# Local attention and a feed-forward layer on one core: scores in four quarters, first loads from two queues, and an ordering list with other numbers

## Chip, core and metric

One core of a Trainium2 chip. The metric is device microseconds of one launch, median of three runs. The engines named here: PE (TensorE; PEld is its weight load), DVE (VectorE), ACT (ScalarE), POOL (GpSimd), SP (SyncE, which begins the DMAs). PSUM has eight banks of 128 x 512 fp32 here.

## What is computed

For 8 batches of 8 heads, 576 tokens and 64 features: attention over q, k, v averaged by four, repeated back to full length, plus attention within three tokens to either side; the sum goes through a layer norm and a two-layer ReLU network and is added to its input.

```python
q_d = q.reshape(B, H, Sd, factor, D).mean(axis=3)        # the same for k and v, factor 4
out_up = np.repeat(sm_attn(q_d, k_d, v_d), factor, axis=2)
mask = np.abs(pos[:, None] - pos[None, :]) < factor
scores = np.where(mask, scale * np.matmul(q, k.transpose(0, 1, 3, 2)), -1000000000.0)
out_local = np.matmul(softmax(scores), v)
x = (out_up + out_local)                                 # to (8, 576, 512)
xn = (x - mu) / np.sqrt(var + 1e-06) * g_ln
out = x + np.maximum(xn @ w_ch1, 0.0) @ w_ch2            # 512 -> 2048 -> 512
```

The network's weights come as float64, 16.8 MB, and its products are made in three passes (hi and lo parts of weights and activations).

## The kernel before

**Windows.** The tokens of a batch are cut into five windows of 2 x 58 queries, 40 windows in all, numbered i. A window's two halves (`par` 0 and 1) lie on partitions 0 to 63 and 64 to 127, and each has 64 keys. `local(i)` adds a window's steps: loads of q and k (names qn, kn for windows 0 to 6, which PE transposes; qr, kr for the others, which DVE transposes in 32 x 32 blocks), the load of v into one of two tiles vwin, scores into PSUM (tile ls), mask, maximum (lmx), subtraction, exp (la), a PE transpose (lt, copied out as at), the product with v (lv), the division (xl), and DMAs that move the rows of xl into the token tiles x of 128 rows.

**Scores.** Windows 0 to 6 use `scores_by_pair`, which writes two banks. The others use `scores` (L473): for each of 8 heads and each half, a product of 64 x 64 by 64 whose inputs and outputs both lie on the half's partitions, into one bank.

**Pooled attention.** `pooled(b)` loads q, k, v (raw), adds fours on POOL, and makes scores gs, transposes gq and gt, and the product gv. Batch 0 takes its sums of q and k from the windows' transposes instead.

**Norm and network.** `norm(n)` adds the pooled part to tile x, normalises it and transposes it on PE (px); ACT writes the hi part (xh, L879), DVE the lo part (xlo). `ffn(c, p)` works on 18 chunks of 256 tokens and 8 pairs of weight blocks: 24 products into h, ReLU on ACT (hh) and the rest on DVE (hl), 12 products into acc. Chunks 0 and 1 run side by side while the weights come in. `weights(which, f)` loads a block of w1 or w2 as two tiles s, and turns it into hi and lo with ACT (cva L328, hi L347), DVE (cva L336 and L339) and DVE or POOL (lo L352).

**Order.** Nothing is ordered by hand. Each step is added to a `Plan` with an engine, a duration in us, a due time, the buffers it takes and gives back (`u`: 87 SBUF units, `a`: the 8 PSUM banks), and a `lag` after which its result counts as there (2.9 us for a load). `Plan.order` (L49) places the steps one after another by these numbers, and every engine runs its instructions in that order. An instruction that waits holds up all that stands behind it on its engine. All DMAs are begun by SP.

```python
t = add("PE", 1.28, scores, turned, due - 6.0, take=A, give=(("u", 2),))
last_local.v[i % 2] = tv = add("PE", 1.3, times_v, (at, vt), due - 1.0, take=(("a", 2),), give=U)
vt = add("SP", 4 * DMA, load_v, (last_local.v[i % 2],), due - 8.0, lag=LAT, ahead=AHEAD)
```

Of the kernel before, what the change touches and what calls it, by code (L numbers as in the profile page):

```python
# [22 lines left out]
class Plan:  # L23
# [25 lines left out]
    def order(self):  # L49
# [40 lines left out]
        while left:  # L90
# [45 lines left out]
def attention_then_ffn(  # L136
# [32 lines left out]
    NPE, NPB = 7, 1  # L169
    SEP = {}  # L170
# [135 lines left out]
    def weights(which, f):  # L306
# [49 lines left out]
        t = add("SP", 2 * DMA, load, (), due, take=(("u", 3),), lag=LAT + 1.0, ahead=W_AHEAD)  # L356
# [16 lines left out]
    def local(i):  # L373
# [18 lines left out]
        def load_rows(src, nm):  # L392
            x.raw[nm] = unit([P, H, D], f"{nm}n{i}")
            for par in range(2):
                t0 = window_start(w, par)
                nc.sync.dma_start(  # L396
# [3 lines left out]
        def load_v():  # L400
            for par in range(2):
                t0 = window_start(w, par)
                for h2 in range(2):
                    nc.sync.dma_start(  # L404
# [7 lines left out]
        for src, nm in ((q, "q"), (k, "k")):  # L412
            if by_pe:
# [35 lines left out]
                t = add("SP", 1.46, lambda src=src, nm=nm: load_rows(src, nm), (), due - 12.0, take=U,  # L449
                        lag=LAT, ahead=AHEAD)  # L450
# [6 lines left out]
            else:  # L457
# [9 lines left out]
                for jb in range(2):  # L467
                    ts.append(add("SP", 4 * DMA, lambda src=src, nm=nm, jb=jb: load_blocks(src, nm, jb), ts,
                                  due - 14.0, take=() if jb else U, lag=LAT, ahead=AHEAD))
                turned.append(add("DVE", dve(512), turn, ts, due - 8.0, take=U, give=U))  # L470
        vt = add("SP", 4 * DMA, load_v, (last_local.v[i % 2],), due - 8.0, lag=LAT, ahead=AHEAD)

        def scores():  # L473
            x.ps = psa(f"ls{i}").rearrange("p (h j) -> p h j", h=H)
            for h in range(H):
                for par in range(2):
                    hs = slice(64 * par, 64 * par + 64)
                    nc.tensor.matmul(x.ps[hs, h], lhsT=x.qt[hs, h], rhs=x.kt[hs, h], start=True, stop=True)  # L478
# [21 lines left out]
        def masked():  # L500
            nc.vector.tensor_add(x.ps, x.ps, mask.unsqueeze(1).broadcast_to([P, H, 64]))

        def largest():
            x.mx = work.tile([P, H], F32, tag="lmx", bufs=6, name=f"lmx{i}")
            nc.vector.reduce_max(x.mx, x.ps, axis=AX.X)
            if not by_dve:
                nc.vector.tensor_single_scalar(out=x.mx, in_=x.mx, scalar=-SCALE, op=ALU.mult)
# [13 lines left out]

        def shifted():
            nc.vector.tensor_sub(x.ps, x.ps, x.mx.unsqueeze(2).broadcast_to([P, H, 64]))

        def exps():
            x.a = unit([P, H, 64], f"la{i}")
            if by_dve:
                nc.scalar.activation(x.a, x.ps, AF.Exp, scale=SCALE)
                return
            for h in range(H):  # L530
                nc.scalar.activation(x.a[:, h], x.ps[:, h], AF.Exp, scale=SCALE, bias=x.mx[:, h : h + 1])
# [24 lines left out]
        def times_v():  # L556

            x.pv = [
                psa(f"lv{i}_{h2}")[:, : NPAIR * (D + 1)].rearrange("p (h e) -> p h e", h=NPAIR)
                for h2 in range(2)  # L560
            ]
            for pr in range(NPAIR):
                for h2 in range(2):
                    js = slice(64 * h2, 64 * h2 + 64)
                    for par in range(2):
                        hs = slice(64 * par, 64 * par + 64)
                        nc.tensor.matmul(  # L567
                            x.pv[h2][hs, pr], lhsT=x.at[js, pr, hs], rhs=vwin[js, par, pr], start=True, stop=True
# [20 lines left out]
        if by_pe:  # L589
            t = add("PE", 1.6, scores_by_pair, turned, due - 6.0, take=(("a", 2),), give=(("u", 2),))  # L590
            t = add("DVE", 2 * dve(256) + (2 * dve(256) if by_dve else 0.15), largest_by_pair, (t,), due - 5.0)
            t = add("ACT", 2 * act(256) if by_dve else 1.6, exps_by_pair, (t,), due - 5.0, take=U, give=(("a", 2),))
        else:
            t = add("PE", 1.28, scores, turned, due - 6.0, take=A, give=(("u", 2),))
            t = add("DVE", dve(512), masked, (t,), due - 5.0)
            t = add("DVE", dve(512) + (0 if by_dve else 0.15), largest, (t,), due - 5.0)
            if by_dve:
                t = add("DVE", dve(512), shifted, (t,), due - 5.0)
            t = add("ACT", act(512) if by_dve else 1.28, exps, (t,), due - 5.0, take=U, give=A)
# [446 lines left out]
```

## Time and profile before

| | |
|---|---|
| median of 3 runs | 1099.75 us (1098.24 to 1103.15) |
| profiled execution | 1100.44 us, span of its instructions 1098.7 us |
| mean granted clock of TensorE | 0.977 |
| instructions | 23266 |
| DMA | 105.35 MB in 262572 packets, 206912 of them under 512 B |

An engine's share of busy time is a mean over stages. The profile is read by stage: the first 64 us, in which batch 0 goes through attention; 64 to about 160 us, in which the weights come in and chunks 0 and 1 run; and the rest, in which chunks 2 to 17 run with the attention of later batches between them. In rows of waits the columns are the engine and line that waited, for whom, us in total, times, and the longest.

### The profile page before, as it was taken

How to read it: one execution, taken by the hardware profiler on the slowest of the kernel's cores; microseconds unless marked ns; L12 is line 12 of the kernel's file. 1: busy time of each engine (PE TensorE's matmuls, PEld its weight loads, DVE VectorE, ACT ScalarE, POOL GpSimd, SP SyncE). 2: the span in 40 equal slices, each digit the busy share in tenths (PEclk: the TensorE clock that was granted, in tenths of full speed). 3: DMA queues.
4: the chain of work that ended last, by engine and by line, in shares of the span. 5: the costliest groups of instructions: out<-in, count | busy, mean ns of one | idle time of the engine just before them, and what ended most of it. 6: DMA issues, size and time to landing. Idle time of an engine off the chain costs nothing.

```text
span 1098.7 us, 23266 instructions
## 1 busy us (share of the span) xinstructions
PE 1053.8 (96%) x9182; PEld 943.5 (86%) x9182; DVE 513.2 (47%) x1212; ACT 313.5 (29%) x828; POOL 265.3 (24%) x275
## 2 busy tenths in 40 slices
PE   8887689999999999999999999999999999999998
PEld 6776579989889898999898999898988989898997
DVE  7679774634343453453435443544424453534211
ACT  5466443322322222232212131322212232212100
POOL 2313565142214140041132322131400500100000
PEclk9689789999999999999999999999999999999999
DMA  7599754364424344234252525333532333311000
GB/s 161 119 246 258 182 135 116 74 148 95 78 71 113 73 109 88 72 81 118 57 128 57 132 54 104 75 109 74 128 80 68 83 83 60 81 26 48 9 20 20
DMA packets 262572, 105.35 MB, mean 96 GB/s; under 512 B 206912, under 2 KB 245056, under 8 KB 262464
## 3 DMA queue, kind: packets, MB, share of 16 engines
q1 hardware_dynamic: 262464, 103.87, 40.1%
q8 instruction: 72, 1.18, 0.5%
q14 instruction: 36, 0.29, 0.1%
HBM read 82.58 MB, written 11.80 MB: 86 GB/s over the span
## 4 chain that ended last, share of the span: by engine, by line
PE 82%; DMA 10%; SPq 3%; DVE 3%; issue 1%; ACT 1%; POOL 0%; DVEq 0%; ACTq 0%
PE h L933 34%; PE acc L956 33%; DMA s<-in_moe_w_ch_dram 5%; PE ls L478 3%; DMA x<-xl 3%; PE gv L761 3%; PE lv L567 2%; PE gs L725 2%; SPq L396 1%; PE lt L547 1%; PE gt L744 1%; PE px L872 1%; SPq L404 1%; DMA raw2k<-in_k_dram 1%; PE gq L698 1%
## 5 line engine op out<-in xcount | busy, mean ns | idle before, releaser
L956 PE MATMUL acc<-hi,hl 128*128 128x512 f32 x576 | 238.6, 414 | 5.1 <-DVE hl L944 5.1
L956 PE MATMUL acc<-lo,hh 128*128 128x512 f32 x576 | 229.1, 398 | 0.3 <-DVE lo L352 0.3
L956 PE MATMUL acc<-hi,hh 128*128 128x512 f32 x576 | 227.2, 394 | 0.0
L944 DVE SCALAR_TENSOR_TENSOR hl<-h,hh 128x512 fp32r<-128x512 f32 x144 | 98.9, 687 | 265.4 <-ACT hh L940 235.4
L940 ACT ACTIVATE hh<-h 128x512 fp32r<-128x512 f32 x144 | 86.1, 598 | 428.7 <-PE h L933 376.7
L933 PE MATMUL h<-xh,lo 128*128 128x256 f32 x1152 | 194.0, 291 | 0.1
L933 PE MATMUL h<-xlo,hi 128*128 128x256 f32 x1152 | 185.7, 284 | 0.0
L933 PE MATMUL h<-xh,hi 128*128 128x256 f32 x1152 | 185.6, 284 | 0.0
L933 PEld LDWEIGHTS h<-xh,lo 128*128 128x128 f32 x1152 | 170.0, 191 | 17.5 <-ACT xh L879 0.3
L933 PEld LDWEIGHTS h<-xlo,hi 128*128 128x128 f32 x1152 | 159.5, 193 | 0.0
L933 PEld LDWEIGHTS h<-xh,hi 128*128 128x128 f32 x1152 | 159.2, 192 | 0.0
L848 POOL TENSOR_TENSOR x<-x,up 128x512 f32<-128x512 f32 x32 | 41.5, 1297 | 377.6 <-DMA x<-xl 187.8
L956 PEld LDWEIGHTS acc<-hi,hh 128*128 128x128 f32 x576 | 109.5, 190 | 25.4
L956 PEld LDWEIGHTS acc<-hi,hl 128*128 128x128 f32 x576 | 110.5, 192 | 21.6 <-DVE hl L944 5.8
L956 PEld LDWEIGHTS acc<-lo,hh 128*128 128x128 f32 x576 | 110.7, 192 | 13.3 <-DVE lo L352 0.6
L879 ACT ACTIVATE xh<-px,gain 128x128 fp32r<-128x128 f32 x144 | 43.9, 371 | 81.1 <-PE px L872 62.0
L889 DVE SCALAR_TENSOR_TENSOR xlo<-px,gain,xh 128x128 fp32r<-128x128 f32 x144 | 43.0, 345 | 41.4 <-ACT xh L879 40.4
L761 PEld LDWEIGHTS gv<-vd,agt 72*72 72x72 f32 x512 | 41.1, 157 | 2.9 <-issue 0.9
L738 ACT ACTIVATE ag<-gs,gmx 96x144 f32<-96x144 f32 x96 | 29.2, 373 | 49.5 <-DVE gmx L730 42.0
L964 DVE SCALAR_TENSOR_TENSOR x<-acc,x 128x512 f32<-128x512 f32 x36 | 24.5, 687 | 38.4 <-PE acc L956 38.4
L761 PE MATMUL gv<-vd,agt 72*72 72x65 f32 x512 | 41.7, 240 | 0.3 <-ACT agt L754 0.3
L339 DVE SCALAR_TENSOR_TENSOR cva<-s,cva 128x256 int32<-128x256 int32 x64 | 40.7, 676 | 1.1
(181 smaller groups left out, 1125.7 us busy)
## 6 DMA issues: line engine op xcount, KB each, us to landing
s<-in_moe_w_ch_dram SPq DMA_DIRECT2D x64, 256.0 KB
vwin<-in_v_dram SPq DMA_DIRECT2D x160, 64.0 KB
out_dram<-x SPq DMA_DIRECT2D x36, 256.0 KB
qr<-in_q_dram SPq DMA_DIRECT2D x264, 32.0 KB
kr<-in_k_dram SPq DMA_DIRECT2D x264, 32.0 KB
up<-ud SPq DMA_DIRECT2D x28, 256.0 KB
x<-xl SPq DMA_DIRECT2D x40, 116.0 KB
ud<-od SPq DMA_DIRECT2D x32, 72.0 KB
```

Source lines behind the costliest of these rows:

```text
L339: nc.vector.scalar_tensor_tensor(out=a, in0=x.raw[i].rearrange("p (n two) -> p n two", two=2)[:, :, 0], scalar=29, in1=a, op0=ALU.logical_ ...
L478: nc.tensor.matmul(x.ps[hs, h], lhsT=x.qt[hs, h], rhs=x.kt[hs, h], start=True, stop=True)
L738: nc.scalar.activation(y.a[:, c], y.ps[:, c], AF.Exp, scale=POOLED_SCALE, bias=y.mx[:, c : c + 1])
L761: nc.tensor.matmul(y.pv[:, qh, h2], lhsT=y.at[kh][:, h2, qh * GH : (qh + 1) * GH], rhs=vd[:, kh, 2 * pr + h2], start=kh == 0, stop=kh == 1,)
L848: (nc.vector if by_pe else nc.gpsimd).tensor_add(xt[n], xt[n], x.up)
L879: nc.scalar.activation(xh[c][i][:, k, j * P : (j + 1) * P], pxt[n][:, kc], AF.Copy, scale=gain[:, kc : kc + 1])
L889: nc.vector.scalar_tensor_tensor(out=xlo[c][i][:, k, ts], in0=pxt[n][:, kc], scalar=gain[:, kc : kc + 1], in1=xh[c][i][:, k, ts].bitcast(F ...
L933: nc.tensor.matmul(ph[c, p][:, fi], lhsT=wt[:, kc], rhs=xx[kc // 2][:, kc % 2], start=n == 0, stop=n == 3 * KC - 1)
L940: nc.scalar.activation(hh[c, p], ph[c, p], AF.Relu)
L944: nc.vector.scalar_tensor_tensor(out=hl[c, p].rearrange("p c t -> p (c t)"), in0=ph[c, p].rearrange("p c t -> p (c t)"), scalar=0.0, in1=h ...
L956: nc.tensor.matmul(acc[c][j], lhsT=lt[:, fi, ts], rhs=rt, start=p == 0 and fi == 0 and n == 0, stop=p == NPR - 1 and fi == 1 and n == 2,)
L964: nc.vector.scalar_tensor_tensor(out=x, in0=acc[c][j], scalar=1.0 + 2.0**-23, in1=x, op0=ALU.mult, op1=ALU.add)
```

## The change

It has three parts.

1. Windows 7 to 39 get `scores_by_block`: the two halves go into two banks, and within a bank the heads of even and odd number go to the two halves of the partitions. So a product reads one half of the partitions and writes either half. Mask, maximum, subtraction and exp go over two banks of 256 columns. The layout is carried on: vwin is loaded with the half on the partitions, and each move of xl rows becomes two DMAs with pieces of 64 floats.
2. The k loads of batch 0 (windows 0 to 4) and the V loads of windows 0 and 1 are begun by ACT.
3. The list's numbers are others, and a running count of bytes at 245 KB per us lengthens the lag of a load.

```diff
@@ Plan
+        self.rate, self.moved = 245.0, 0.0
...
+            if t.kb:
+                self.moved = max(self.moved, t.start) + t.kb / self.rate
+                t.lag = max(t.lag, self.moved - t.end + t.lag - 1.0)
@@ numbers
     def act(n, sbuf=False):
-        return ((112 if sbuf else 61) + n) / 1200.0
+        return (0.155 if sbuf else 0.14) + n / 1430.0
...
-        t = add("SP", 2 * DMA, load, (), due, take=(("u", 3),), lag=LAT + 1.0, ahead=W_AHEAD)
+        t = add("SP", 2 * DMA, load, (), due, take=(("u", 3),), lag=LAT, kb=512, ahead=W_AHEAD)
...
-                add("PE", 1.31, lambda fi=fi: up(fi),
+                add("PE", 1.44, lambda fi=fi: up(fi),
...
-                "PE", 1.3, lambda fi=fi: down(fi), (t, wdone[2, 2 * p + fi], prev),
+                "PE", 1.38, lambda fi=fi: down(fi), (t, wdone[2, 2 * p + fi], prev),
@@ queues
+    NVA = 2
...
-                t = add("SP", 1.46, lambda src=src, nm=nm: load_rows(src, nm), (), due - 12.0, take=U,
-                        lag=LAT, ahead=AHEAD)
+                eng, queue = ("ACT", nc.scalar) if own and nm == "k" else ("SP", nc.sync)
+                t = add(eng, 1.35, lambda src=src, nm=nm, queue=queue: load_rows(src, nm, queue), (), due - 12.0, take=U,
+                        lag=LAT, kb=256, ahead=AHEAD)
...
-        vt = add("SP", 4 * DMA, load_v, (last_local.v[i % 2],), due - 8.0, lag=LAT, ahead=AHEAD)
+        eng, queue = ("ACT", nc.scalar) if i < NVA else ("SP", nc.sync)
+        vt = add(eng, 3.4 if own else 4 * DMA, lambda: load_v(queue), (last_local.v[i % 2],), due - 8.0, lag=LAT, kb=256, ahead=AHEAD)
@@ scores
-        def scores():
-            x.ps = psa(f"ls{i}").rearrange("p (h j) -> p h j", h=H)
-            for h in range(H):
-                for par in range(2):
-                    hs = slice(64 * par, 64 * par + 64)
-                    nc.tensor.matmul(x.ps[hs, h], lhsT=x.qt[hs, h], rhs=x.kt[hs, h], start=True, stop=True)
+        def scores_by_block():
+            x.ps = [
+                psa(f"ls{i}_{par}")[:, : NPAIR * 64].rearrange("p (c j) -> p c j", c=NPAIR) for par in range(2)
+            ]
+            for pr in range(NPAIR):
+                for par in range(2):
+                    hs = slice(64 * par, 64 * par + 64)
+                    for h2 in range(2):
+                        nc.tensor.matmul(
+                            x.ps[par][64 * h2 : 64 * h2 + 64, pr], lhsT=x.qt[hs, 2 * pr + h2], rhs=x.kt[hs, 2 * pr + h2],
+                            start=True, stop=True,
+                        )
...
+        t = add("PE", 0.75, scores_by_pair if by_pe else scores_by_block, turned, due - 6.0,
+                take=(("a", 2),), give=(("u", 2),))
+        if not by_pe:
+            t = add("DVE", dve(256), lambda: masked(0), (t,), due - 5.0)
+            t = add("DVE", dve(256), lambda: masked(1), (t,), due - 5.0)
...
-        last_local.v[i % 2] = tv = add("PE", 1.3, times_v, (at, vt), due - 1.0, take=(("a", 2),), give=U)
+        last_local.v[i % 2] = tv = add("PE", 0.7, times_v, (at, vt), due - 1.0, take=(("a", 2),), give=U)
@@ move
-                nc.sync.dma_start(xt[n][p0 : p0 + m], x.xl[r0 : r0 + m].rearrange("p h d -> p (h d)"))
+                to = xt[n][p0 : p0 + m]
+                if by_pe:
+                    r0 += 64 * par
+                    nc.sync.dma_start(to, x.xl[r0 : r0 + m].rearrange("p h d -> p (h d)"))
+                    return
+                for h2 in range(2):
+                    nc.sync.dma_start(
+                        to.rearrange("p (c h d) -> p h c d", c=NPAIR, h=2)[:, h2],
+                        x.xl[64 * h2 + r0 : 64 * h2 + r0 + m].rearrange("p (c n) d -> p n c d", n=2)[:, par],
+                    )
```

What this does to the order of instructions is shown at three places. A row has the line, the operation, what it writes and reads, and the shape; a number behind a name tells tiles of the same name apart.

SP in the first microseconds, before (the last q and k loads of batch 0, then v of windows 0 and 1, pooled v, and the first blocks of w1):

```order
L396 DMA qn_227<-in_q_dram 64x8x64 x2
L396 DMA kn_259<-in_k_dram 64x8x64 x2
L404 DMA vwin_77<-in_v_dram 64x4x64 x4
L659 DMA raw0v_326<-in_v_dram 72x4x256
L404 DMA vwin_78<-in_v_dram 64x4x64 x4
L659 DMA raw0v_367<-in_v_dram 72x4x256
L316 DMA s_0_0_391<-in_moe_w_ch_dram 128x2x256
L316 DMA s_0_1_392<-in_moe_w_ch_dram 128x2x256
```

The same place now, and behind it ACT's first instructions now:

```order
L401 DMA qn_161<-in_q_dram 64x8x64 x2
L670 DMA raw0v_186<-in_v_dram 72x4x256
L670 DMA raw0v_199<-in_v_dram 72x4x256
L321 DMA s_0_0_212<-in_moe_w_ch_dram 128x2x256
L321 DMA s_0_1_213<-in_moe_w_ch_dram 128x2x256
L321 DMA s_1_0_243<-in_moe_w_ch_dram 128x2x256
L321 DMA s_1_1_244<-in_moe_w_ch_dram 128x2x256
L401 DMA qn_260<-in_q_dram 64x8x64 x2
L401 DMA kn_270<-in_k_dram 64x8x64 x2
L326 DMA s_0_0_291<-in_moe_w_ch_dram 128x512
```

```order
L233 ACT_TABLE_LOAD
L233 CAST ident_b<-ident 128x128
L401 DMA kn_111<-in_k_dram 64x8x64 x2
L401 DMA kn_117<-in_k_dram 64x8x64 x2
L401 DMA kn_126<-in_k_dram 64x8x64 x2
L416 DMA vwin_77<-in_v_dram 64x4x64 x4
L439 COPY lqt_197<-lq_136 128x512
L439 COPY lkt_201<-lk_149 128x512
L401 DMA kn_216<-in_k_dram 64x8x64 x2
L401 DMA kn_252<-in_k_dram 64x8x64 x2
```

The five k loads and the first V loads have left SP, and the first blocks of both weights and the q and k of window 5 (qn_260, kn_270) follow the q loads there.

ACT around its first hi parts of normalised tokens (xh), before:

```order
L347 CAST hi_0_726<-cva_0_568 128x512
L347 CAST hi_1_730<-cva_1_594 128x512
L554 COPY at_789<-lt_775 128x512
L586 ACTIVATE xl_791<-lv_1_750,lr_1_793 128x64 x4
L586 ACTIVATE xl_843<-lv_1_797,lr_1_845 128x64 x4
L427 COPY lqt_875<-lq_866 128x512
L879 ACTIVATE xh_0_888<-px_879,gain 128x128 x2
```

And now (the number in front of the last one of hi and cva is the weight block f):

```order
L333 ACTIVATE cva_5_914<-s_5_1_529 128x256
L439 COPY lqt_926<-lq_921 128x512
L439 COPY lkt_933<-lk_928 128x512
L352 CAST hi_2_970<-cva_2_853 128x512
L592 ACTIVATE xl_979<-lv_1_949,lr_1_1001 128x64 x4
L439 COPY lqt_1026<-lq_1007 128x512
L439 COPY lkt_1029<-lk_1016 128x512
L333 ACTIVATE cva_4_1035<-s_4_0_849 128x256
L333 ACTIVATE cva_4_1035<-s_4_1_850 128x256
L890 ACTIVATE xh_0_1054<-px_1044,gain 128x128 x2
```

Ahead of the first xh stood the conversions of blocks 0 and 1 of w1 alone; now those of blocks 0 to 5 of w1 and 0 to 4 of w2 are begun there (eleven pairs of cva, seven hi), and the transposes' copies of windows 5 and 6 are done.

PE at the scores of window 7, before:

```order
L744 MATMUL gt_0_1_2523<-ident,ag_0_2502 72x96 x3
L478 MATMUL ls_2529<-lkt_2383,lqt_2381 64x64 x16
L933 MATMUL h_7_2555<-xh_0_1009,lo_14_2324 128x256 x2
L933 MATMUL h_7_2555<-xh_1_1019,lo_14_2324 128x256 x2
L933 MATMUL h_7_2555<-xh_0_1009,hi_14_2250 128x256 x2
```

And now:

```order
L944 MATMUL h_7_2528<-xlo_1_1262,hi_14_1975 128x256 x2
L517 MATMUL ls_0_2543<-lkt_2403,lqt_2395 64x64 x2
L517 MATMUL ls_1_2544<-lkt_2403,lqt_2395 64x64 x2
L517 MATMUL ls_0_2543<-lkt_2403,lqt_2395 64x64 x2
L517 MATMUL ls_1_2544<-lkt_2403,lqt_2395 64x64 x2
L517 MATMUL ls_0_2543<-lkt_2403,lqt_2395 64x64 x2
```

The sixteen products of a window stay sixteen; they go by twos into the one bank and the other.

More of the change, by code (lines that the diff above doesn't have):

```diff
@@ L35, in __init__, with add @@
         self.lags = (80, 0.3, 0.6)
-    def add(self, eng, dur, fn, deps=(), due=0.0, take=(), give=(), lag=None, ahead=1e9, alt=None):
+        self.rate, self.moved = 245.0, 0.0
+    def add(self, eng, dur, fn, deps=(), due=0.0, take=(), give=(), lag=None, ahead=1e9, alt=None, kb=0):
         opts = {eng: (dur, fn, 0.0)}
@@ L43, in add @@
             n=len(self.tasks), opts=opts, dur=dur, deps=[d for d in deps if d is not None],
-            due=due, take=take, give=give, lag=lag, ahead=ahead, open=0.0, waits=0, eng=None, fn=None,
+            due=due, take=take, give=give, lag=lag, ahead=ahead, open=0.0, waits=0, eng=None, fn=None, kb=kb,
         )
@@ L498, in scores_by_pair, with masked @@
                         )
[L500 to L507, printed above, removed]
+        def scores_by_block():
[10 more added lines that the diff above has]
+                        )
+        def masked(n):
+            nc.vector.tensor_add(x.ps[n], x.ps[n], mask.unsqueeze(1).broadcast_to([P, NPAIR, 64]))
         def largest_by_pair():
@@ L520, in largest_by_pair @@
                 )
[L522 to L531, printed above, removed]
         def exps_by_pair():
@@ L588, in local @@
         by_dve = i in SHIFTED or i >= LATE
[L589 to L599, printed above, removed]
+        t = add("PE", 0.75, scores_by_pair if by_pe else scores_by_block, turned, due - 6.0,
+                take=(("a", 2),), give=(("u", 2),))
+        if not by_pe:
+            t = add("DVE", dve(256), lambda: masked(0), (t,), due - 5.0)
+            t = add("DVE", dve(256), lambda: masked(1), (t,), due - 5.0)
+        t = add("DVE", 2 * dve(256) + (2 * dve(256) if by_dve else 0.15), largest_by_pair, (t,), due - 5.0)
+        t = add("ACT", 2 * act(256) if by_dve else 1.6, exps_by_pair, (t,), due - 5.0, take=U, give=(("a", 2),))
         t = add("PE", 0.43, turn_a, (t,), due - 3.0, take=A, give=U)
         at = add("ACT", act(512), turn_a_out, (t,), due - 3.0, take=U, give=A)
-        last_local.v[i % 2] = tv = add("PE", 1.3, times_v, (at, vt), due - 1.0, take=(("a", 2),), give=U)
+        last_local.v[i % 2] = tv = add("PE", 0.7, times_v, (at, vt), due - 1.0, take=(("a", 2),), give=U)
         outs = []
         for h2 in range(2):
-            t = add("DVE", 0.24, lambda h2=h2: inverse(h2), (tv,), due)
+            t = add("DVE", 0.28, lambda h2=h2: inverse(h2), (tv,), due)
             outs.append(
@@ L675, in pooled_half @@
                 by_dve = b == 0 and nm == "k"
-                t = add("SP", 0.82, load, (), due - 4.0, take=STG, lag=LAT, ahead=AHEAD)
+                t = add("SP", 0.82, load, (), due - 4.0, take=STG, lag=LAT, kb=288, ahead=AHEAD)
                 t = add(
-                    "DVE" if by_dve else "POOL", dve(512) + dve(256) if by_dve else 2.02,
+                    "DVE" if by_dve else "POOL", dve(512) + dve(256) if by_dve else 2.1,
                     (lambda key=key: pool4(key, nc.vector)) if by_dve else pool4, [t, lastg.vd[hg] if nm == "v" else None] + ready.get(nm, []),
@@ L804, in pooled_pair @@
                             take=U if own else (), give=A))
-        t = add("PE", 0.97, times_v, outs + ready["v"], due - 1.0, take=A, give=(("u", 2),) if own else ())
+        t = add("PE", 1.04, times_v, outs + ready["v"], due - 1.0, take=A, give=(("u", 2),) if own else ())
         lastg.v = lastg.vd[hg] = t
@@ L900, in norm @@
             t = add("SP", DMA * len(rows), load_up, [d for _, _, b, _ in rows for d in ud_done[b]], due - 4.0,
-                    take=U, lag=LAT, ahead=12.0)
+                    take=U, lag=LAT, kb=256, ahead=12.0)
             t = add("POOL", pool(512), plus, [t] + piece[n], due - 3.0, give=U)
-        t = add("DVE", 0.95, stats, (t,), due - 1.0)
-        t = add("POOL", 0.46, rstd, (t,), due - 1.0)
+        t = add("DVE", 1.1, stats, (t,), due - 1.0)
+        t = add("POOL", 0.52, rstd, (t,), due - 1.0)
         t = add("DVE", 0.46, normed, (t,), due, take=U, ahead=12.0)
@@ L992, in ffn @@
                 t = add("DVE", dve(512), lambda j=j: finish(j), (prev,), due + 1.5 * PACE, give=A)
-                add("SP", DMA, lambda j=j: store(j), (t,), due + 2 * PACE, give=U, lag=LAT + 0.7)
+                add("SP", DMA, lambda j=j: store(j), (t,), due + 2 * PACE, give=U, lag=LAT + 0.7, kb=256)
     plan.add("POOL", 2.5, make_masks, (), 0.0)
```

48 lines of the change are left out of this document (27 added, 21 removed).

## The prediction

> **What bounds the kernel now.** I read the page's busy shares and its chain first, then the busy time by stage, then who waits for whom in the stage where TensorE (PE) stands still.
>
> ```profile
> PE 1053.8 (96%) x9182; PEld 943.5 (86%) x9182; DVE 513.2 (47%) x1212; ACT 313.5 (29%) x828; POOL 265.3 (24%) x275
> PE 82%; DMA 10%; SPq 3%; DVE 3%; issue 1%; ACT 1%; POOL 0%; DVEq 0%; ACTq 0%
> PE h L933 34%; PE acc L956 33%; DMA s<-in_moe_w_ch_dram 5%; PE ls L478 3%; DMA x<-xl 3%; PE gv L761 3%; PE lv L567 2%; PE gs L725 2%; SPq L396 1%; PE lt L547 1%; PE gt L744 1%; PE px L872 1%; SPq L404 1%; DMA raw2k<-in_k_dram 1%; PE gq L698 1%
> ```
>
> 82% of the chain that ended last is PE, and nearly all the DMA in it is weights and x pieces. So what PE executes costs its own time, and every other engine costs only where PE waits for it. The next rows say where that is: stretch in us, its length, busy time of PE, PEld, DVE, ACT and POOL, granted clock, DMA share, GB/s.
>
> ```profile
> 0.00:60.00 60.00, 45.30 (x562) 39.05 (x562) 39.42 (x135) 30.36 (x88) 15.80 (x28) 0.85 0.63 145
> 80.00:100.00 20.00, 15.63 (x121) 13.38 (x120) 17.67 (x27) 11.99 (x27) 8.43 (x7) 0.91 0.92 263
> 100.00:120.00 20.00, 13.41 (x105) 11.09 (x104) 17.39 (x36) 12.64 (x35) 7.33 (x7) 0.92 1.03 255
> 160.00:1080.00 920.00, 913.90 (x7966) 823.21 (x7965) 386.44 (x917) 225.14 (x588) 205.13 (x209) 1.00 0.36 82
> 64.00:160.00 96.00, 76.08 (x531) 65.46 (x530) 80.93 (x146) 54.66 (x145) 43.63 (x37) 0.87 0.80 205
> 0.00:64.00 64.00, 48.92 (x605) 42.04 (x606) 43.03 (x147) 32.47 (x93) 16.58 (x29) 0.83 0.64 153
> ```
>
> Two stages with different limits. From 160 on PE is busy 913.9 of 920 us at clock 1.00: there a microsecond off PE is a microsecond off the kernel. From 64 to 160 PE idles 96 - 76.1 = 19.9 us and its clock is 0.87, while the DMA engines are full until 120 and DVE is busy 81 of 96. Before 64 nothing is full: DMA moves 145 to 153 GB/s where it can do 263.
>
> **Part 1: local scores in four quarters.** Windows 7 to 39 are 33, all begun after 196 us, in the stage that PE bounds. One window's scores before, and a product that is four-quartered already and has the same shape (64 rows, 64 columns, 65 streamed instead of 64), each between its neighbours:
>
> ```profile
> 346.59 0.64 PE L933 MATMUL h<-xlo,hi 128*128 128x256 f32 x4
> 347.16 1.15 PE L478 MATMUL ls<-lkt,lqt 64*64 64x64 f32 x32
> 348.24 0.35 PE L698 MATMUL gq<-ident,qd 72*128 72x72 f32 x2
> 333.06 0.64 PE L933 MATMUL h<-xlo,hi 128*128 128x256 f32 x4
> 333.63 0.70 PE L567 MATMUL lv<-vwin,at 64*64 64x65 f32 x32
> 334.25 0.74 PE L933 MATMUL h<-xh,lo 128*128 128x256 f32 x4
> ```
>
> Starts give occupancy: scores hold PE from 347.16 to 348.24, 1.08 us; the values product, with as many instructions (32), from 333.63 to 334.25, 0.62 us. The new scores step through the quarters in the order in which that product does, so I price them at 0.62. Gain 0.46 us a window, 33 x 0.46 = **15.2 us**. The chain agrees: 3% for 33 score groups is 1.0 us each, 2% for 40 value groups 0.55.
>
> What it adds lies on DVE: mask, maximum and subtraction now go over two banks of 256 columns each.
>
> ```profile
> L505 DVE TENSOR_REDUCE lmx<-ls 128x8 f32<-128x512 f32 x33 | 22.5, 682 | 0.5
> L512 DVE TENSOR_REDUCE lmx<-ls 128x4 f32<-128x256 f32 x14 | 5.2, 413 | 0.0
> ```
>
> Two of 413 ns instead of one of 682 are 0.14 us more; three such operations a window make 0.43, x 33 = 14 us of DVE in a stage where DVE is busy 386 of 920. I cost it at nothing; the cover is PE's own work. With the cover gone it costs at most 0.43 us a window. The scores also hold two PSUM banks instead of one; the order counts banks, so this shows as a group moved, not as a wait.
>
> **Part 2: the windows' results move in 256-byte pieces.** Rows of xl were 2 KB; now each row is eight pieces, and each move is two DMAs.
>
> ```profile
> q1 hardware_dynamic: 262464, 103.87, 40.1%
> L624 SPq DMA_DIRECT2D x<-xl x112: 575/738/2098, 29.0 to 1017.2; - x112
> 17.74 2.46 DMA vwin<-in_v_dram
> 42.79 8.78 DMA x<-xl
> 286.97 7.62 DMA x<-xl
> ```
>
> Of the 112 moves, 92 belong to windows 7 and up, so 92 more issues of 0.74 us: 68 us of SP, spread over some 800 us. 33 windows' 3,800 rows become 30,400 packets, 26,600 more. At the mean packet of q1 (0.401 x 16 x 1098.7 us over 262,464 packets: 27 ns) that is 26,600 x 27 ns / 16 = 45 us of the 16 engines, 5% of a stage in which they are used 36%. V loads already travel in 256-byte pieces and landed in 2.46 us where x pieces took 7.62 to 8.78 in traffic. I cost it at nothing; POOL's add of x stands behind these moves and PE's transposes of x behind that, which is the second rival below.
>
> The Trainium skill, "DMA: Bandwidth & Descriptors", section "Specifications", puts the least transfer for line rate at 512 B, and so speaks against these pieces. By it the moves would take longer than I allow; the rows of V do not show that at 64 KB, and no row of this trace shows an x move in pieces.
>
> **Part 3: loads begun from ACT, and the new order of the start.** Ten k loads and eight V loads leave SP, where the q, k and V issues stand in one line until 18 us.
>
> ```profile
> L396 SPq DMA_DIRECT2D qn<-in_q_dram x14: 607/635/849, 1.3 to 69.8; - x14
> L404 SPq DMA_DIRECT2D vwin<-in_v_dram x160: 595/612/1477, 15.8 to 971.3; - x160
> L328 ACT ACTIVATE cva<-s 128x256 f32<-128x256 f32 x64 | 26.7, 438 | 23.7 <-DMA s<-in_moe_w_ch_dram 23.2
> L347 ACT CAST hi<-cva 128x512 fp32r<-128x512 f32 x32 | 19.3, 621 | 14.4 <-DVE cva L339 14.4
> 64.68 1.11 PE L933 MATMUL h<-xh,lo 128*128 128x256 f32 x4
> ```
>
> No DMA is begun from ACT in this trace, so I price an issue there as on SP: 10 x 0.635 + 8 x 0.612 = 11.3 us. By the order rows, ACT also converts more weights ahead of its first xh: eleven pairs of cva instead of two and seven hi instead of two, 18 x 0.44 + 5 x 0.62 = 11.0 us. Together 22.3 us more ahead of the first xh, on an engine busy 32.5 of the first 64 us. It fits into the idle 31.5 us if ACT's waits shrink; nothing is left for h to start sooner than 64.7. So I leave h's start where it is: gain 0, bounds -9 (all idle time but the 22.3 gone) and +22.3 (no idle time used).
>
> What the earlier weights are worth is read from the waits between 64 and 160:
>
> ```profile
> PE acc L956 <- DVE hl L944: 5.1, 2, 4.3
> PE gs L725 <- ACT ktg L711: 4.3, 1, 4.3
> PE ls L486 <- ACT lqt L427: 4.3, 1, 4.3
> PE gt L744 <- ACT ag L738: 3.3, 2, 2.7
> PE lv L567 <- ACT at L554: 2.1, 1, 2.1
> ACT cva L328 <- DMA s<-in_moe_w_ch_dram: 17.5, 23, 2.7
> ACT hi L347 <- DVE cva L339: 14.4, 7, 4.6
> ```
>
> PE waits 19.1 us, nearly always for a short ACT or DVE step that stands in its engine's line behind a weight conversion. That conversion waits 17.5 us for the weight's DMA and 14.4 us for DVE. Loads that are issued earlier cure the first kind; the second is DVE's own load (81 of 96 us), which the change does not lighten. The first kind is 17.5 of 31.9, 55%, and I take that share of PE's waits: 0.55 x 19.1 = **10.5 us**. Bounds: 0, and 19.1 plus half of what the slow clock costs there (0.13 x 96 = 12.5 us at most), together 25.
>
> The Trainium skill, same page, section "Issuing engines are not separate DMA queues", says that beginning transfers on several engines saves only the sequencer's time. By it the move to ACT is worth at most the 11.3 us of issuing; the 0.63 DMA share of the first 60 us agrees that issuing, not the wire, was short there.
>
> **Part 4: the order after 160.** The list's numbers for PE, ACT and DVE groups and a running count of bytes reorder everything after.
>
> ```profile
> PE px L872 <- DVE xn L862: 3.9, 2, 2.9
> PE lt L547 <- ACT la L531: 1.5, 1, 1.5
> ```
>
> These two are nearly all that PE waits after 165. They may vanish or others come; I take 0, bounds -6 and +6.
>
> **Sum.** The profiled execution took 1100.44 us, 1.7 above its span and 0.7 above the median of the runs. 1100.4 - 15.2 - 10.5 = 1074.7, so 1075.
>
> **The rivals.**
> *The start pays nothing* (chance 0.20). New waits take the place of the old, because DVE is as full as before. For it: 81 of 96 us. Against it: by the order two pairs of weight blocks are converted before the first xh and a third is begun. 1100.4 - 15.2 = 1085.
> *The x pieces come late* (0.05), the slower end. Place: PE's transposes of x, twice a chunk. The trace has this wait twice, up to 2.9 us, behind an x move of 7 us. If the split moves land later than POOL's add has slack, each of the 15 chunks after the first three waits 2.9 us: +43, 1118. It decides the sign from eleven such chunks on (31 us). Against it: DMA share 0.36.
> *ACT is late at the start* (0.05). Ahead of its first xh ACT has 22.3 us more and in-order waits for weights; if none of its idle time is used, and the old waits stay, 1100.4 - 15.2 + 22.3 = 1107.5 (0.01 of the 0.05; the rest with two thirds of the delay, near 1100). It shows as h beginning at 80 us or later.
> *The start pays in full* (0.15): all 19.1 and half the clock's 12.5: 1100.4 - 15.2 - 19.1 - 6.2 = 1060.
> *The quarters do not overlap* (0.05): scores stay at 1.08 us: 1100.4 - 10.5 = 1090. The values product speaks against it.
>
> **How the numbers follow.** The forecast, 1075, has the other 0.50. A measurement of this kernel tells about 0.5%, 5.5 us, from no change. Faster by more: forecast, both cases of the start and unsplit quarters, 0.90; within: the milder late ACT, 0.04; slower: late x and late ACT, 0.06. The range 1060 to 1090 takes in the forecast, the start at nothing and at nearly all, and leaves out some 0.15.
>
> **What would show it.** Scores at 0.62 us from start to start, and their chain share at 2% or less: part 1. h beginning between 58 and 72 us, PE's waits from there to 160 near 9 us, ACT's waits for weights' DMA well under 17.5 us: part 3. PE after 165 idle about 6 us: part 4; if px waits grow in most chunks, part 2 was wrong. The forecast fails upward if DVE, not DMA, paces the weights, and downward if the slow clock goes with the waits.

## The result and the profile after

The changed kernel is **slower**: 1110.91 us, median of five runs (1107.35 to 1118.34), beside 1098.24 us before (1095.98 to 1103.15). The ratio is 1.0105, 95% interval 1.0075 to 1.0134. The forecast was 1075, the range 1060 to 1090. The profiled execution took 1108.08 us, with a span of 1106.0 and a mean granted clock of 0.969 (before: 1100.44, 1098.7 and 0.977).

The page of the changed kernel: busy time by engine, and the chain that ended last by engine and by line.

```profile
PE 1039.0 (94%) x9182; PEld 929.7 (84%) x9182; DVE 508.4 (46%) x1308; ACT 310.6 (28%) x852; POOL 264.5 (24%) x274
PE 75%; DMA 11%; SPq 5%; DVE 4%; issue 2%; ACT 1%; POOL 1%; DVEq 0%; ACTq 0%; POOLq 0%
PE h L944 31%; PE acc L967 31%; DMA x<-xl 4%; PE gv L772 3%; SPq L632 2%; PE lv L573 2%; PE gs L736 2%; PE ls L517 2%; PE gt L755 1%; DMA s<-in_moe_w_ch_dram 1%; PE lt L552 1%; DMA qn<-in_q_dram 1%; PE px L883 1%; DMA raw5v<-in_v_dram 1%; DVE cva L344 1%
```

PE is busy 1053.8 - 1039.0 = 14.8 us less, what the scores were to save. But PE's idle time, span less busy, grew from 44.9 to 67.0 us, by 22.1. In the chain SP's issues of x moves (L632) now have 2%, where the rows of before named none, and the landing of x went from 3% to 4%. The same kernel by stage, columns as before:

```profile
0.00:64.00 64.00, 41.97 (x520) 34.84 (x520) 39.34 (x128) 32.80 (x94) 15.99 (x27) 0.85 0.93 183
64.00:160.00 96.00, 72.52 (x554) 64.23 (x555) 73.26 (x159) 48.58 (x134) 35.36 (x32) 0.81 0.62 177
160.00:1080.00 920.00, 902.21 (x7981) 811.19 (x7980) 392.36 (x1017) 227.47 (x623) 213.14 (x216) 0.99 0.38 83
```

PE's idle time before 160 us went from 15.1 + 19.9 = 35.0 to 22.0 + 23.5 = 45.5, **10.5 us more where 10.5 less was forecast**. After 160 it went from 6.1 to 17.8, **11.7 more where nothing was forecast**. Less the 14.8 us of busy time, that is the span's growth of 7.3, but for the rounding and the ends of the windows. So there are two losses to find, one at the start and one after it. PE's timeline first, then its waits from 64 to 160 us:

```profile
81.84 1.20 PE L944 MATMUL h<-xh,lo 128*128 128x256 f32 x4
...
355.32 0.69 PE L517 MATMUL ls<-lkt,lqt 64*64 64x64 f32 x32
355.94 0.34 PE L709 MATMUL gq<-ident,qd 72*128 72x72 f32 x2
```

```profile
PE acc L967 <- DVE hl L955: 7.8, 1, 7.8
PE lt L552 <- ACT la L547: 6.5, 1, 6.5
PE lv L573 <- DVE cva L341: 6.2, 1, 6.2
```

The scores take 355.94 - 355.32 = 0.62 us, as priced. The first network product begins at 81.84 instead of 64.68, and what PE waits for is again ACT and DVE, in three long pieces. ACT's timeline shows two candidates for the start, its issues (ACTq) and what stands ahead of xh:

```profile
2.24 5.77 ACTq L401 DMA_DIRECT2D kn<-in_k_dram  x5
8.55 4.63 ACTq L416 DMA_DIRECT2D vwin<-in_v_dram  x4
13.27 0.58 ACT L439 COPY lqt<-lq 128x512 f32<-128x512 f32 x1 [10.89 <-DMA vwin<-in_v_dram]
...
15.27 6.43 ACTq L401 DMA_DIRECT2D kn<-in_k_dram  x4
25.91 4.86 ACTq L416 DMA_DIRECT2D vwin<-in_v_dram  x4
...
76.91 0.43 ACT L333 ACTIVATE cva<-s 128x256 f32<-128x256 f32 x1 [4.28 <-DMA s<-in_moe_w_ch_dram]
77.51 0.43 ACT L333 ACTIVATE cva<-s 128x256 f32<-128x256 f32 x1 [0.17 <-DMA s<-in_moe_w_ch_dram]
77.84 2.15 ACT L890 ACTIVATE xh<-px,gain 128x128 fp32r<-128x128 f32 x8
```

The issues take 22.4 us of ACT with the first one (0.71), not 11.3, and the first copy waits until 13.27 (before: 7.60). Later the first xh, at 77.84, stands behind conversions that wait 4.28 us for a weight's DMA. How far the input of xh was late by itself is seen on DVE and PE, where xn is x after the norm (first the kernel before, then two rows of the changed one):

```profile
53.31 0.54 DVE L862 TENSOR_SCALAR xn<-x,mv 128x512 f32<-128x512 f32 x1
...
71.17 0.54 DVE L873 TENSOR_SCALAR xn<-x,mv 128x512 f32<-128x512 f32 x1
72.23 0.64 PE L883 MATMUL px<-ident,xn 128*128 128x128 f32 x4
```

The first xn is 17.9 us late. PE has its transpose done at 72.87, and xh starts 5.0 us after that; before, xh followed at once (54.91 and 54.95). So the queue on ACT straight ahead of xh holds 5.0 of the 22.9 us by which xh is late, and the rest lies ahead of xn. DVE, too, has more weights there: 23 of its weight instructions (cva and lo) start before the first xn, against 6 before.

After 160 one wait stands out in PE's row, 3.9 us before, and the chain around the longest case shows how it comes about (start, us, what):

```profile
PE px L883 <- DVE xn L873: 10.3, 5, 7.2
```

```profile
824.35 0.89 SPq L632
...
825.29 0.84 SPq L632
...
826.18 0.66 SPq L632
...
826.88 0.69 SPq L632
...
827.68 1.04 SPq L632
...
828.77 5.15 DMA x<-xl
...
835.61 0.56 DVE xn L873
...
836.30 1.09 PE px L883 x4
```

SP issues five moves one after another (4.4 us from first to last end), the last lands 5.15 us later, then DVE normalises x and PE transposes it.

### The profile page after: what moved, and what is told of

It reads as the page before. It is cut to its first block, busy times and chain, and to the rows that moved or that the text cites. A ratio compares the mean times of both kernels' runs of the same rounds, so it can differ in the third digit from the quotient of the medians.

```text
span 1106.0 us, 23604 instructions
## 1 busy us (share of the span) xinstructions
PE 1039.0 (94%) x9182; PEld 929.7 (84%) x9182; DVE 508.4 (46%) x1308; ACT 310.6 (28%) x852; POOL 264.5 (24%) x274
## 4 chain that ended last, share of the span: by engine, by line
PE 75%; DMA 11%; SPq 5%; DVE 4%; issue 2%; ACT 1%; POOL 1%; DVEq 0%; ACTq 0%; POOLq 0%
PE h L944 31%; PE acc L967 31%; DMA x<-xl 4%; PE gv L772 3%; SPq L632 2%; PE lv L573 2%; PE gs L736 2%; PE ls L517 2%; PE gt L755 1%; DMA s<-in_moe_w_ch_dram 1%; PE lt L552 1%; DMA qn<-in_q_dram 1%; PE px L883 1%; DMA raw5v<-in_v_dram 1%; DVE cva L344 1%
## 5 line engine op out<-in xcount | busy, mean ns | idle before, releaser
L967 PEld LDWEIGHTS acc<-hi,hl 128*128 128x128 f32 x576 | 110.1, 191 | 23.8 <-DVE hl L955 8.2
L863 DVE BATCH_NORM_STATS2 st<-x 128x6 f32<-128x512 f32 x36 | 24.8, 689 | 78.6 <-POOL x L859 78.4
L552 PE MATMUL lt<-ident,la 128*128 128x128 f32 x160 | 25.6, 284 | 20.2 <-ACT la L547 10.2
L573 PE MATMUL lv<-vwin,at 64*64 64x65 f32 x1280 | 30.5, 229 | 12.6 <-DVE cva L341 6.2
L573 PEld LDWEIGHTS lv<-vwin,at 64*64 64x64 f32 x1280 | 24.3, 138 | 20.0 <-DVE cva L341 6.4
```

The lines of the kernel that those rows point to most:

```text
L552: nc.tensor.transpose(x.pt[:, pr * P : (pr + 1) * P], x.a[:, 2 * pr : 2 * pr + 2].rearrange("p h j -> p (h j)"), ident,)
L573: nc.tensor.matmul(x.pv[n][hs, pr], lhsT=x.at[js, pr, hs], rhs=vwin[js, m, pr], start=True, stop=True)
L863: nc.vector.bn_stats(st, xt[n])
L967: nc.tensor.matmul(acc[c][j], lhsT=lt[:, fi, ts], rhs=rt, start=p == 0 and fi == 0 and n == 0, stop=p == NPR - 1 and fi == 1 and n == 2,)
```

## The experiments

Theory of the start: the order brings weights ahead of x (**order**), against ACT standing in its DMA issues (**issues**). Theory of the rest: the moves in 256-byte pieces (**pieces**), against the new numbers of the list. Ratios are to the kernel before on the same chip, with 95% intervals.

### The parts apart

Four kernels: the changed one with its 18 loads back on SP (`a_loads_back`), and the kernel before with the loads on ACT alone (`b_loads_only`), with the scores, V layout and moves alone (`c_scores_only`), and with the numbers and the byte count alone (`d_numbers_only`).

```diff
# a_loads_back
-                eng, queue = ("ACT", nc.scalar) if own and nm == "k" else ("SP", nc.sync)
+                eng, queue = "SP", nc.sync
-    NVA = 2
+    NVA = 0
# c_scores_only: a_loads_back, and in it the old numbers, e.g.
-        self.rate, self.moved = 245.0, 0.0
+        self.rate, self.moved = 1e12, 0.0
-        return (0.155 if sbuf else 0.14) + n / 1430.0
+        return ((112 if sbuf else 61) + n) / 1200.0
```

> The changed kernel with the first batch's k loads and the two V loads begun by SP again; scores in quarters and the list's numbers stay. Theory Q (the wire is full of 256-byte pieces, and the second queue makes ACT stand in its own DMA issues): ACT's evictions of the first window come at about 8 us again instead of 13, the first h at 62 to 70 us instead of 82, and 1108 falls by 10 to 20 us to 1088 to 1098. Rival N (the new numbers and the count of bytes put weights ahead of x and so delay h): h still begins at 75 us or later and the time stays within 5 us of 1108.

> The kernel before with nothing but the ten k loads and eight V loads moved to ACT; scores and numbers as before. Theory Q: ACT stands in its issues for about 20 us where SP's rows said 11.3, the first h comes at 72 us or later instead of 64.7, and the time is 5 to 15 us above the kernel before. Rival N: no change within 3 us, or a little faster, as q and k are issued sooner.

> The kernel before with the scores of windows 7 to 39 in four quarters (with their V layout and split moves), old numbers elsewhere and all loads on SP, so that the first 64 us are in the order of before. If the 15.2 us of PE reach the end: 1083 to 1087. If the split moves and their double issues on SP bring waits of PE at px (theory M): PE's waits after 165 us grow from 6 to 12 or more, and the time is 1088 to 1095.

> The list's new numbers and the count of bytes alone: scores, moves and queues as before. If the numbers cure waits as the prediction had it, PE waits less than 19 us between 64 and 160 and the time is 1085 to 1095. If they are what costs (rival N), 1100 to 1115 with h after 70 us. If they neither help nor cost, 1095 to 1103.

| | median us | ratio to before | first h at, us | weight conversions (cva) ahead of the first xh on ACT |
|---|---|---|---|---|
| before | | | 64.68 | 4 |
| changed | 1110.91 | 1.0105 (1.0075 to 1.0134) | 81.84 | 22 |
| a_loads_back | 1105.31 | 1.0057 (1.0032 to 1.0081) | 65.40 | 2 |
| b_loads_only | 1122.02 | 1.0207 (1.0182 to 1.0233) | 84.19 | 18 |
| c_scores_only | 1099.35 | 0.9994 (0.9974 to 1.0015) | 63.26 | 4 |
| d_numbers_only | 1099.29 | 0.9993 (0.9973 to 1.0014) | 67.02 | 2 |

The numbers by themselves change nothing. The loads on ACT cost 2.1% by themselves, more than the 5 to 15 us expected, and h is late wherever they are there. The scores with their moves gain nothing and lie above both of the ranges expected for them, though PE's busy time fell to 1042.8 us: something in this part gives their gain back. With the loads back on SP h is early again, but the kernel stays slower than before, 1105.31 where 1088 to 1098 was expected. `a_loads_back` and `c_scores_only` differ in the numbers alone, and their intervals lie apart: beside the split moves the new numbers cost 0.6%. PE's row of waits for xn after 165 us, of `a_loads_back` and of `c_scores_only`:

```profile
PE px L883 <- DVE xn L873: 18.0, 6, 7.9
```

```profile
PE px L883 <- DVE xn L873: 9.2, 6, 3.9
```

Both are above the 3.9 us of before. The profiled execution of `c_scores_only` is its fastest, 1093.59 us, so its row may show too little.

### Same order, other engine for the loads

The first table can't tell issues from order, since both come with the loads on ACT. Here the plan is made as in the changed kernel, so that every engine has exactly its order, but the 18 loads are begun by SP or by POOL.

```diff
-                eng, queue = ("ACT", nc.scalar) if own and nm == "k" else ("SP", nc.sync)
+                eng, queue = ("ACT", nc.sync) if own and nm == "k" else ("SP", nc.sync)
-        eng, queue = ("ACT", nc.scalar) if i < NVA else ("SP", nc.sync)
+        eng, queue = ("ACT", nc.sync) if i < NVA else ("SP", nc.sync)
```

> The changed kernel with the eighteen loads begun by SP while every engine keeps the changed kernel's order of instructions (ACT has all of its others in the same order). Theory Q (ACT stands in its own DMA issues while the wire is full): with the issues gone from ACT, its first eviction comes at 7 to 9 us, the first h at 65 to 74 us and the time falls by 8 to 18 us to 1092 to 1102. Rival N (the order, weights ahead of x, is what delays): first h at 78 us or later and 1105 to 1115.

> The same, with the eighteen loads begun by POOL, so that two engines begin loads at once as in the change but ACT is free. Theory Q with ACT as the victim: first h at 66 to 76 us and 1092 to 1103. If the two queues' packets themselves harm each other (rival W: q's first pieces land later because k, V and weights share the wire), the first q lands later than 5.5 us as in the change, evictions come at 10 us or later though ACT is free, and the time stays above 1105.

By SP: 1115.67 us, ratio 1.0130 (1.0103 to 1.0157). By POOL: 1113.74, 1.0117 (1.0091 to 1.0143). ACT's and PE's timelines of the run with SP:

```profile
7.10 0.59 ACT L439 COPY lqt<-lq 128x512 f32<-128x512 f32 x1 [4.71 <-DVE gsq L454]
```

```profile
83.76 1.20 PE L944 MATMUL h<-xh,lo 128*128 128x256 f32 x4
```

ACT's first copy is back at 7.10 us, and h still begins at 83.76; by POOL they come at 8.10 and 83.86. So the 22.4 us of issues on ACT are not what delays h, and this falls as a cause. Nor does it take a second queue: h is as late with SP's alone. This leaves the order, which a later run tests directly.

### The moves alone

The kernel before, same order, with the moves of windows 7 to 39 as two DMAs of 256-byte pieces (`f_moves_only`); the scores alone with a longer lag of the moves in the plan, 7.0 instead of 2.9 us, so that the list allows for late moves (`g_moves_lag_old`); and, since the first does two things at once, the kernel before with two DMAs for each move that carry 1 KB of a row each (`p_moves_two_rows`).

```diff
# f_moves_only
-                nc.sync.dma_start(xt[n][p0 : p0 + m], x.xl[r0 : r0 + m].rearrange("p h d -> p (h d)"))
+                for h2 in range(2):
+                    nc.sync.dma_start(
+                        xt[n][p0 : p0 + m].rearrange("p (c h d) -> p h c d", c=NPAIR, h=2)[:, h2],
+                        x.xl[r0 : r0 + m].rearrange("p (c h) d -> p h c d", h=2)[:, h2],
+                    )
# p_moves_two_rows
+                for c2 in range(2):
+                    nc.sync.dma_start(
+                        xt[n][p0 : p0 + m, 256 * c2 : 256 * (c2 + 1)],
+                        x.xl[r0 : r0 + m, 4 * c2 : 4 * (c2 + 1)].rearrange("p h d -> p (h d)"),
+                    )
```

> The kernel before, same scores, same numbers and so the same order of instructions, but the moves of windows 7 to 39 as two DMAs with pieces of 64 floats. If theory M holds (the split moves and their second issue on SP make x late), PE's waits at px after 165 us grow from 3.9 to 7 or more and the time is 4 to 12 us above the kernel before. If the moves are hidden, within 3 us of it.

> The run with scores in quarters alone (1099 median), with one number changed: the list counts a move as there after 7.0 us instead of 2.9. If waits at px ate the scores' gain (theory M), they fall below 4 us after 165 and the time is 1085 to 1092. If the gain went elsewhere, 1096 to 1102 as without it.

> The kernel before, same order, with the moves of windows 7 to 39 as two DMAs each as in the run with the moves alone, but cut by columns of the row: each moves one run of 1 KB per row instead of four pieces of 256 bytes. Theory that SP's second issue costs the time (0.7 to 0.8 us more for each of the 92 moves ahead of the loads behind them): 1114 to 1124 us as the 256-byte pieces gave (1120), SP's issues of moves at 3% of the chain after 165 us. Theory that the 256-byte pieces cost it (they land late, or the wire is taken): 1098 to 1105. Half of each: 1106 to 1113.

The pieces: 1120.22 us, ratio **1.0170** (1.0138 to 1.0203). Two DMAs of 1 KB runs: 1103.07 us, ratio **1.0027** (1.0009 to 1.0045). For each, the issues of these moves on SP (min, median, max in ns), PE's waits after 165 us, and the last issue and landing of the chain at the same place of the program. First the pieces:

```profile
L628 SPq DMA_DIRECT2D x<-xl x184: 613/806/2183, 213.1 to 1043.5; - x184
PE px L879 <- DVE xn L869: 13.2, 4, 6.0
310.97 2.18 SPq L628
...
313.20 4.59 DMA x<-xl
```

Then the 1 KB runs:

```profile
L628 SPq DMA_DIRECT2D x<-xl x184: 575/706/957, 210.8 to 1019.9; - x184
PE px L879 <- DVE xn L869: 6.1, 3, 3.8
307.55 0.57 SPq L628
...
308.17 5.68 DMA x<-xl
```

Both issue 184 DMAs instead of 92, and that alone costs 0.27%. The rest, 1.4%, goes with the pieces; all of it is 18.5 us, where 4 to 12 were expected. An issue takes 806 ns at the median instead of 706, and 26 of the 184 take over 1.5 us, none of the same moves with 1 KB runs or before. Added up over the trace, these moves hold SP for 172.1 us, against 127.9 with 1 KB runs and 67.7 before, and they stand in one line, so that the last one of a burst is late. At the place shown the landing itself takes no longer (4.59 against 5.68 us), and all packets together took 39.8% of the 16 DMA engines with pieces, 39.5% with 1 KB runs and 40.1% before. So the rows point to SP's issues and not to the wire; no run here moves the issues away and keeps the pieces. Of the run with pieces the span is 23.8 us above that of before: 13.2 of it is more idle time of PE, and 10.6 more busy time for the same instructions (1064.4 against 1053.8), at a mean clock of 0.965 instead of 0.977. I read this as the waits costing once more in clock; that the waits cause the clock was not tested by itself.

A longer lag in the plan gave 1106.8 us, 1.0049 (1.0026 to 1.0071): the waits of px fell to 4.7 us, but the plan also moved the start (first h at 71.69). Because both changed, and the time lies above both of the ranges expected, this run decides nothing on the lag.

### Whole rows, and weights that begin later

If the pieces eat the scores' gain, xl must leave in whole rows. For windows 7 to 39 each half of the division is done in two instructions on 64 partitions, which put all eight heads of a query on one partition, and a move is one DMA of 2 KB rows again. This is put into `c_scores_only` (`k_scores_whole`) and into `a_loads_back` (`l_loads_back_whole`). For the start, the changed kernel with its loads on ACT gets one line that keeps weight loads from beginning ahead of 30 in the plan (`m_weights_at_30`), and `n_whole_act_at_30` has both.

```diff
# k, l and n: division and move
+                parts = [(slice(64 * m, 64 * m + 64), slice(64 * h2, 64 * h2 + 64), m) for m in range(2)]
+            for src, dst, hh in parts:
+                xl = x.xl[dst].rearrange("p (c h) d -> p h c d", h=2)[:, hh]
...
-                for h2 in range(2):
-                    nc.sync.dma_start(
-                        to.rearrange("p (c h d) -> p h c d", c=NPAIR, h=2)[:, h2],
-                        x.xl[64 * h2 + r0 : 64 * h2 + r0 + m].rearrange("p (c n) d -> p n c d", n=2)[:, par],
-                    )
+                r0 += 64 * par
+                nc.sync.dma_start(to, x.xl[r0 : r0 + m].rearrange("p h d -> p (h d)"))
# m and n: in weights(which, f), behind the load
+        if f >= 0:
+            t.open = 30.0
```

> The scores in quarters as in the run with the scores alone (old numbers, loads begun by SP), but xl is written in whole rows: for windows 7 to 39 each half of the division is done in two pieces of 64 partitions, and a move is one DMA of 2 KB rows again. Theory that the moves in 256-byte pieces eat what the scores save: 1083 to 1092 us against about 1100 before, waits of px for xn after 165 us at most 6 us (9.2 with the pieces, 3.9 before), SP's issues of moves no longer in the chain. Rival, the scores' saving is lost in the order of the work or in the clock and not in the pieces: 1096 to 1103, waits of px still 9 or more. Rival, 66 more divisions cost VectorE and ScalarE what the moves give back: 1096 or more, with px or lt waiting for VectorE outside of the moves.

> The changed kernel with its 18 first loads begun by SP again and xl written in whole rows (numbers and scores of the change kept). If the pieces cost here what they cost in the kernel before (about 10 to 18 us): 1087 to 1095 us, first h at 65 to 68. If they cost nothing beside the new numbers: 1102 to 1108 as with the loads alone put back (1105.3).

> The changed kernel with its loads begun by ScalarE and its moves in pieces, and one line more: no expert weight load may begin before 30 in the list's plan, so that 4 weight conversions instead of 22 stand ahead of the first xh on ScalarE. Theory that the order (weights pulled ahead of x) delays h: first h at 64 to 71 us, time 1095 to 1105. Rival, the 18 loads on ScalarE or the wire full of 256-byte pieces delay h: first h at 78 or later, 1108 or more. A third case: h is early but weights are then late, PE waits for w in 70 to 160 us, 1105 to 1112.

> Both together: the changed kernel with the weight loads from 30 in the plan and xl in whole rows. If the two costs are separate and add up: 1080 to 1092 us, below both kernels, first h at 64 to 71. If the loads on ScalarE cost something by themselves: above the run with the loads begun by SP and whole rows by 5 us or more.

| | moves in pieces | whole rows |
|---|---|---|
| scores alone | c: 1099.35, 0.9994 (0.9974 to 1.0015) | k: 1087.69, 0.9894 (0.9852 to 0.9937) |
| changed, loads on SP | a: 1105.31, 1.0057 (1.0032 to 1.0081) | l: 1081.23, 0.9847 (0.9808 to 0.9885) |
| changed, loads on ACT, weights from 30 | m: 1099.41, 1.0001 (0.9983 to 1.0019) | n: **1080.80, 0.9817** (0.9776 to 0.9859) |

Across each row the pieces are worth 1.0%, 2.1% and 1.8%; the intervals of each pair lie apart. The kernels with whole rows also have the other division and its durations in the list, so their order is not quite the same; the comparison in one order is `f_moves_only` against before. `l_loads_back_whole` came out below the 1087 to 1095 us expected. PE's waits for xn after 165 us of `k` and `l` (9.2 and 18.0 with pieces):

```profile
PE px L881 <- DVE xn L871: 4.2, 4, 1.6
```

```profile
PE px L881 <- DVE xn L871: 0.5, 1, 0.5
```

That 66 more divisions would cost as much as the moves, the second rival of that run, is excluded by k.

Now the start. `m` differs from the changed kernel by the two lines shown and is 11.5 us faster by the medians. By stage, ACT's and PE's timelines, and the waits for xn that stay:

```profile
0.00:64.00 64.00, 44.22 (x562) 38.13 (x563) 32.15 (x122) 24.46 (x73) 14.49 (x27) 0.85 0.77 132
64.00:160.00 96.00, 81.85 (x610) 71.75 (x609) 81.55 (x174) 59.47 (x159) 34.11 (x29) 0.87 0.78 217
160.00:1065.00 905.00, 885.93 (x7842) 795.37 (x7841) 384.83 (x1009) 224.04 (x616) 210.35 (x214) 0.99 0.38 84
67.79 1.12 ACT L892 ACTIVATE xh<-px,gain 128x128 fp32r<-128x128 f32 x4
77.79 1.22 PE L946 MATMUL h<-xh,lo 128*128 128x256 f32 x4
PE px L885 <- DVE xn L875: 9.7, 5, 6.5
```

PE's idle time before 160 us is 19.8 + 14.2 = 34.0, against 45.5 in the changed kernel: 11.5 us less, as much as the medians differ (1.0% by the ratios; the two profiled spans differ by 8.0), and after 165 the waits for xn are what they were (9.7 against 10.3). With 4 conversions instead of 22 ahead of it the first xh came at 67.79 instead of 77.84. So the order is the cause at the start. This run does not part three things that come with the order: the conversions on ACT ahead of xh; those on DVE ahead of the first xn, 23 in the changed kernel and none here, where xn starts at 61.67; and the wire, which was filled to a DMA share of 0.93 in the first 64 us and is at 0.77 now. But my expectation of h between 64 and 71 missed: h began at 77.79, since now the weights are late (ACT waits up to 7.4 us for one), and PE had attention to do in between. The start of h is a poor measure of the loss; the stage's idle time is the measure.

`n`, with both edits, takes 1.8% less than before and has the lowest median here, though it is not told apart from `l`, which has its loads on SP and no held weights (1080.80 and 1081.23 on the same chip). Its stages:

```profile
0.00:64.00 64.00, 45.93 (x570) 39.62 (x570) 32.40 (x122) 24.89 (x74) 14.51 (x27) 0.81 0.78 135
64.00:160.00 96.00, 83.58 (x635) 73.47 (x636) 81.84 (x175) 59.68 (x160) 37.22 (x32) 0.91 0.80 224
160.00:1065.00 905.00, 896.72 (x7941) 805.92 (x7940) 420.11 (x1077) 225.99 (x618) 208.66 (x213) 1.00 0.36 83
```

Idle time is 30.5 us before 160, 8.3 after, and the clock after 160 is 1.00 again.

## Why the prediction was wrong

**What bounds the kernel: right.** PE after 160, and PE's waits for ACT and DVE ahead of it. A gain of PE time did become a gain of the kernel, once nothing else was spoiled: k is 11.8 us below before.

**Part 1, the scores: right.** 0.62 us a window and 2% of the chain as forecast, 14.8 us of PE's busy time for 15.2. The rival that the quarters don't overlap is out. DVE's added work hid for the most part: in `k`, whose DVE is busy 535.1 us instead of 513.2, 11.8 of the 14.8 us reach the end.

**Part 2, the moves in 256-byte pieces: the first step that failed, "I cost it at nothing".** It cost 1.0 to 2.1% of the kernel, some 11 to 23 us. I reasoned with means: 68 us more of SP over 800 us, 5% of engines used at 36%. SP's share was too small as well: 104 us more (172.1 against 67.7, with the pieces alone). And the moves come in bursts of four or five that stand in SP's one line, with a chain of POOL, DVE and PE behind the last. A mean share says nothing of that; the row of 7.62 us for a landing x piece already stood in the chain that ended last. V loads of the same piece size were no evidence for a burst at whose end something waits. The rival "the x pieces come late" had the right place, PE's transposes of x, and 0.05; its size, 2.9 us in each of 15 chunks, was the wrong shape: five waits, the longest 7.2 us. The Trainium skill, "DMA: Bandwidth & Descriptors", section "Specifications", puts the least transfer for line rate at 512 B, and I set that aside for the V loads' row. The outcome here agrees: moves in 256-byte pieces cost 1.70%, the same bytes in as many DMAs of 1 KB runs 0.27%. But the rows point to SP's issues, and not to a longer landing (4.59 against 5.68 us).

**Part 3, the start: the second step that failed, "I leave h's start where it is", and with it the 10.5 us.** I had counted from the order that 18 more cva and 5 more hi stand ahead of the first xh, 11.0 us, and let them vanish in ACT's idle time. An engine that runs in order does not use idle time that way: a conversion waits for its weight's DMA, 4.28 us for the last pair, with xh behind it. That is 5.0 of the 22.9 us by which xh was late; the other 17.9 stand ahead of xn, which I had not priced at all. Holding the weights back took 9.5 of those away (xn at 61.67 in `m`); what share the conversions on DVE, the later attention steps and the wire each have, and what the 8.4 us come from that stay in `m`, is open. So earlier loads gave later products, and PE's idle time before 160 rose by 10.5 us instead of falling by it. The 10.5 us took a share of PE's waits by the kinds of ACT's waits, and supposed that earlier loads cure the first kind. Between 64 and 160 they did not, in sum: the conversions' waits below are 33.4 us instead of 31.9, since one of them is now put down to a move of xl, 8.9 us, and PE idled 23.5 us there instead of 19.9.

```profile
ACT hi L352 <- DVE cva L344: 14.4, 11, 3.0
ACT cva L333 <- DMA s<-in_moe_w_ch_dram: 10.1, 8, 4.3
ACT cva L333 <- DMA x<-xl: 8.9, 1, 8.9
```

The rival "ACT is late at the start" forecast this sign (h after 80 us, 1107.5), at 0.05. That its 1107.5 lies near the measured 1110.91 is luck, as it has nothing in it for the moves. Of its two terms the issues were wrong in size (22.4 us for 11.3) and cost nothing that shows: with them on SP or POOL the time is no lower. The Trainium skill, "DMA: Bandwidth & Descriptors", section "Issuing engines are not separate DMA queues", gave the move at most the time of issuing. The runs agree: in the same order the ratios were 1.0105 with ACT, 1.0130 with SP and 1.0117 with POOL, with intervals that overlap.

**Part 4, the order after 160: right at nothing** by the numbers alone (0.9993), though not beside the split moves, where they cost 0.6% (`a` against `c`). The 11.7 us more of idle time there belong to part 2 for the most part: from 160 to 1065 `m` still idles 905 - 885.9 = 19.1 us, `n` with whole rows 8.3. The order has its share in such waits too: `b`, with whole rows in another order, waits 10.2 us for xn after 165.

**The chances.** Two edits whose cost no row of the trace bounded were set at nothing, and 0.90 was given to faster. The bounds in the text, +22.3 and +43, were not carried into the range.

## What to carry to other kernels

Where an edit makes transfers finer on a path with someone waiting at its end, price the last transfer of a burst, with the issues ahead of it in its line, and not the mean load. When work is moved off a busy queue, look at what the scheduler then pulls forward, and at what stands behind that on every engine that runs in order. A saving on the bounding engine can be real and still be spent elsewhere: compare its idle time by stage before the saving is given up.

## What had not been expected of the hardware

- Five DMAs begun by ACT, beside those that SP began, took 5.77 us, up to 1.9 us from one start to the next, though an issue takes 0.60 to 0.79 us. In the same order SP alone began two in 1.31 us at first, and POOL four in 2.89 us. It did not show in the time here.
- A move in 256-byte pieces takes SP 806 ns to issue at the median, and 26 of 184 take 1.5 to 2.2 us; one of the same bytes in 1 KB runs takes 706 and at most 957.
- A kernel with waits of some us on PE runs the same 9182 matmuls in more busy time: 1064.4 us at a granted clock of 0.965, against 1053.8 at 0.977.
